# A spectral filter and a GELU network on one core: ten tiles' sums kept instead of eight, side-by-side copies of leftover rows, and a new written order

## The chip, the cores and the metric

The kernel runs on one NeuronCore of a Trainium2 chip, as one launch. The metric is the device time of that launch in microseconds (us). Five engines work in parallel, each through its own instructions in order: TensorE (PE, matmuls; its weight loads are shown as PEld), VectorE (DVE), ScalarE (ACT), GpSimd (POOL) and SyncE (SP), which issues nearly all the transfers.

## The reference

The input x has 2048 rows of 640 numbers in bfloat16. It is normalised by row, and the result is the sum of x, of a spectral filter of the normalised rows and of a two-layer network of the same rows:

```python
xn = _layernorm(x, axis=-1)
# A: X = rfft2(xn) over rows and columns, X * (w_r + i w_i), irfft2 back, cast to bf16
# B: h = gelu(xn @ w1 + b1), with w1 640 x 1536;  h @ w2 + b2, with w2 1536 x 640
return x + _A_ref(xn, A_w_r, A_w_i) + _B_ref(xn, B_w1, B_b1, B_w2, B_b2)
```

## The kernel before

The 2048 rows are 16 tiles of 128 rows, row 16p + c lying in tile c on partition p. Everything on PE is a matmul with a 128x128 stationary operand (or a 32-row piece of one), and all of PE's work goes through the helper on line 410, so the profile shows PE by what goes in and out of it, not by line.

*The network.* The first layer runs over seven blocks of tiles (`BLOCKS`: tiles 0, 1, 2-3, 4-5, 6-7, 8-11, 12-15) and 12 chunks of 128 hidden units. `h5.7.0` is block 5, chunk 7, inner slices from 0: three matmuls `ps<-xnT,W`; `h5.7.3` is the other two. ACT applies the GELU (`ge5.7`, line 639). The second layer of a tile is 12 matmuls of 384 columns and 12 of 256 (`CUTS`), `ps<-W,gT`, written in trios: `l9.384.3` is tile 9, the columns from 384, chunks 3 to 5. What the first-layer results sit in is called a bank: PSUM has eight, numbered 0 to 7, and each name in `SLOTS` is given one. `xb`, `Y`, `os` and the like have slots in SBUF in the same list.

*The filter.* The transform over columns and rows is a chain of matmul stages, each with a copy or products behind it. `G` does the first part of the transform over rows (copies `gx` into XV). `b0` to `b5` do the transform over columns, one for each of six `GROUPS` of 3, 3, 2, 3, 3 and 2 tiles (24 or 16 matmuls, `ps<-EB,XV`; copies `xb`). `c0` to `c3` finish the transform over rows with 32x32 matmuls (copies `y`), DVE multiplies with the filter (`m`, lines 690 and 693, and `z`, line 699), `d0` to `d3` go back over the rows (`ps<-T,ntab`; copies `u`), and sixteen transposing transfers `vt0` to `vt15`, issued by SP on line 705, turn the result into XV. `e0` to `e5` (24 or 16 matmuls, `ps<-getab,XV`) are the way back over the columns, group by group; each needs all sixteen turns. Behind an `e` stand copies `yo` and sums `y2` and `yf`, and then for each tile a last matmul `fin` (`ps<-Wf,htab`), DVE's final addition `os` (line 806) and the transfer `out` (line 813).

In `b` and `e` the 160 frequencies do not fit 128 partitions. Each tile has four matmuls of 128 rows and four of 32 rows, the leftover rows, which sit together in the fifth slice of XV, rows of four sorts on four groups of 32 partitions.

*Kept and unkept tiles.* For a tile in `KEEP` the second-layer sums (`k` instead of `l`) are copied out of PSUM early, with x added (`kk`, line 796), into 32-bit space in xnT that the first layer has finished with. Its bank is then free; `fin` later goes to a fresh bank and `os` adds the two. For the others `l` and `fin` share one bank, which is held until `os`.

*Order and waits.* The order on each engine is not found at run time: `ORDER` writes it out, engine by engine, `SLOTS` gives the buffers, and a planner (`Plan`) only derives from the two which semaphore each instruction waits for. Each PSUM bank and slot is reused in the order written, so an instruction may wait for data, or for the last reader of the slot it writes.

## Time and profile before

| | |
|---|---|
| time before, median of 3 runs | 149.14 us (148.47 to 150.26) |
| time of the profiled execution | 148.87 us |
| its span, first to last instruction | 147.5 us |
| mean granted TensorE clock | 1.000 |
| PE busy | 141.7 us (96% of the span) |
| PE weight loads busy | 99.8 us (68%) |
| DVE busy | 114.7 us (78%) |
| ACT busy | 79.3 us (54%) |
| POOL busy | 7.2 us (5%) |

The time of a run is longer than the span by 1.37 us in this execution, which lies around it. [...] In a timeline of the trace a row gives the start, the length, the engine, what is written and read, and the number of instructions merged into it; the time between the starts of two rows, divided by the count of the first, is the pace.

### The profile page before, as it was taken

The page shows a single profiled execution, that of the slowest core. Times are in us where ns is not written, and L with a number is a line of the kernel's source. Part 1 is how long each engine was busy: PE and PEld are TensorE (multiplying, and loading weights), DVE is VectorE, ACT ScalarE, POOL GpSimd, SP SyncE. Part 2 cuts the span into 40 slices and gives each one's busy share as a digit, 9 for nine tenths or more (in the row PEclk, how much of TensorE's full clock was granted, in tenths as well). Part 3 has the DMA queues.
Part 4 walks back from the last instruction along what each step waited for, and adds up shares of the span by engine and source line. Part 5 has one row for each costly group of instructions (what it writes and reads, how often), then busy time and mean ns, then how long its engine had stood idle before and what let it go on. Part 6 is the DMA issues. An engine that isn't in the chain of part 4 may idle for free.

```text
span 147.5 us, 4149 instructions
## 1 busy us (share of the span) xinstructions
PE 141.7 (96%) x1751; PEld 99.8 (68%) x1760; DVE 114.7 (78%) x264; ACT 79.3 (54%) x149; POOL 7.2 (5%) x24
## 2 busy tenths in 40 slices
PE   7999999999999999999999999999899999999993
PEld 7899898886478867455364434446686786667882
DVE  2999999999997555798988999410488789296993
ACT  3659998979755734577795767655242102300000
POOL 2030204112000000000000000000000000000000
PEclk9999999999999999999999999999999999999999
DMA  4999869887999899000007685669001022012225
GB/s 135 306 354 408 142 141 343 145 101 137 293 155 160 221 201 266 16 4 0 7 0 57 126 118 99 103 131 94 2 0 49 0 78 102 5 44 89 89 93 178
DMA packets 29226, 18.40 MB, mean 125 GB/s; under 512 B 20248, under 2 KB 27928, under 8 KB 29080
## 3 DMA queue, kind: packets, MB, share of 16 engines
q1 hardware_dynamic: 29184, 18.14, 54.2%
q8 instruction: 14, 0.23, 0.6%
q14 instruction: 4, 0.03, 0.1%
q10 hardware_dynamic: 24, 0.00, 0.0%
HBM read 10.92 MB, written 2.62 MB: 92 GB/s over the span
## 4 chain that ended last, share of the span: by engine, by line
PE 86%; DMA 4%; ACT 3%; DVE 2%; SPq 2%; issue 1%
PE ps L410 85%; DMA XV<-U 2%; SPq L705 2%; ACT Xb L420 2%; DMA X<-in_A_x_dram 2%; DVE U L521 1%; ACT U L420 1%; PE ps L567 1%; ACT gT L639 0%; DVE T L553 0%; DVE W L806 0%; DVE mv L523 0%; DVE rstd L527 0%
## 5 line engine op out<-in xcount | busy, mean ns | idle before, releaser
L410 PE MATMUL ps<-W,gT 128*128 128x256 bf16 (+3 forms) x396 | 59.3, 296 | 0.0
L410 PE MATMUL ps<-xnT,W 128*128 128x256 bf16 (+2 forms) x411 | 55.5, 286 | 1.2 <-issue 1.1
L410 PEld LDWEIGHTS ps<-W,gT 128*128 128x128 bf16 x396 | 36.9, 98 | 15.4 <-issue 1.2
L410 PEld LDWEIGHTS ps<-xnT,W 128*128 128x128 bf16 x420 | 34.5, 98 | 16.0 <-issue 2.8
L639 ACT ACTIVATE gT<-ps,b1col 128x256 bf16<-128x256 f32 (+2 forms) x84 | 37.6, 524 | 10.3 <-PE ps L410 10.0
L420 ACT ACTIVATE Wf<-ps 128x960 bf16<-128x960 f32 (+1 forms) x8 | 6.7, 869 | 19.2 <-PE ps L410 15.7
L521 DVE BATCH_NORM_STATS2 U<-X 128x6 f32<-128x320 bf16 x32 | 14.1, 473 | 2.1 <-DMA X<-in_A_x_dram 2.1
L420 ACT ACTIVATE T<-ps 128x644 bf16<-128x644 f32 (+2 forms) x17 | 9.3, 580 | 4.7 <-PE ps L410 4.7
L796 DVE TENSOR_TENSOR xnT<-ps,X 128x384 f32<-128x384 f32 (+1 forms) x16 | 7.6, 486 | 4.8 <-PE ps L410 4.8
L806 DVE TENSOR_TENSOR W<-ps,xnT 128x384 bf16<-128x384 f32 (+1 forms) x16 | 7.5, 485 | 4.7 <-PE ps L410 4.5
L420 ACT ACTIVATE XV<-ps 128x1280 bf16<-128x1280 f32 (+1 forms) x8 | 9.6, 1202 | 2.0 <-PE ps L410 2.0
L421 DVE CAST Wf<-ps 128x960 bf16<-128x960 f32 (+1 forms) x4 | 4.3, 1073 | 7.1 <-PE ps L410 7.1
L584 DVE TENSOR_TENSOR T<-T 128x128 bf16<-128x128 bf16 (+1 forms) x32 | 8.9, 315 | 0.1
L806 DVE TENSOR_TENSOR W<-ps,X 128x384 bf16<-128x384 f32 (+3 forms) x17 | 7.6, 465 | 1.7 <-PE ps L410 1.6
L410 PE MATMUL ps<-Wf,htab 128*128 128x384 bf16 (+3 forms) x33 | 8.6, 296 | 0.0
L410 PE MATMUL ps<-getab,XV 32*128 32x160 bf16 (+1 forms) x128 | 7.5, 242 | 0.5 <-DMA XV<-U 0.5
L420 ACT ACTIVATE Xb<-ps 128x960 bf16<-128x960 f32 x5 | 6.2, 1260 | 3.4 <-PE ps L410 3.4
L410 PEld LDWEIGHTS ps<-getab,XV 32*128 32x128 bf16 (+1 forms) x128 | 6.7, 146 | 1.7 <-DMA XV<-U 0.8
L420 ACT ACTIVATE U<-ps 128x512 bf16<-128x512 f32 (+2 forms) x13 | 5.3, 475 | 4.4 <-PE ps L410 4.4
L699 DVE TENSOR_TENSOR T<-T 128x644 bf16<-128x644 bf16 x16 | 7.3, 487 | 0.2
L410 PE MATMUL ps<-EB,XV 32*128 32x160 bf16 (+1 forms) x128 | 7.2, 232 | 0.2 <-ACT Xb L420 0.2
L532 POOL TENSOR_TENSOR rstd<-ve,mhalf 128x2 f32<-128x2 f32 (+1 forms) x8 | 6.1, 758 | 26.6 <-DVE ve L531 26.6
(56 smaller groups left out, 124.6 us busy)
## 6 DMA issues: line engine op xcount, KB each, us to landing
out_dram<-W SPq DMA_DIRECT2D x15, 160.0 KB, 1.8
X<-in_A_x_dram SPq DMA_DIRECT2D x7, 320.0 KB, 5.8
W<-in_B_w_dram SPq DMA_DIRECT2D x10, 192.0 KB, 4.7
W<-in_B_w_dram SPq DMA_DIRECT2D x2, 960.0 KB, 7.0
Wf<-in_A_w_r_dram SPq DMA_DIRECT2D x7, 160.5 KB, 5.5
Wf<-in_A_w_i_dram SPq DMA_DIRECT2D x7, 160.5 KB, 3.8
gtab<-c_G SPq DMA_DIRECT2D x1, 512.0 KB, 7.5
htab<-c_H SPq DMA_DIRECT2D x1, 512.0 KB, 6.1
```

The lines of the kernel that those rows point to most:

```text
L410: ins = e.matmul(o_, lhsT=lw, rhs=rh, start=st, stop=sp_, skip_group_check=True)
L420: return e.activation(dst(), src(), ACT.Copy)
L421: return e.tensor_copy(dst(), src())
L521: K.op(f"st{c}.{h}", "dve", lambda e, _, c=c, h=h: e.bn_stats(stats[:, c, 6 * h:6 * h + 6], view(X, c * D + H2 * h, [[1, H2]])), reads=[B_ ...
L532: K.op(f"rs{c0}", "pool", lambda e, _, a=a, b=b: e.tensor_tensor(out=rstd[:, a:b], in0=ve[:, a:b], in1=mhalf[:, a:b], op=ALU.pow), reads=[ ...
L567: ins = e.transpose(psb(tps.slot, [[1, 512]]).bitcast(BF)[:, 128 * j:128 * j + 128], xnv(n, 128 * j, [[1, 128]]), ident)
L584: ring_ops.append(K.op(f"f2{pair}.{k}{i}", "dve", lambda e, _, op=op, x1v=x1v, xfv=xfv, o_=o_, o0=o0, o1=o1, w=w: e.tensor_tensor(out=xfv( ...
L639: K.op(f"ge{bi}.{fc}", "act", lambda e, _, c0=c0, nt=nt, fc=fc, f0=f0, hps=hps: e.activation(gT[:, fc, 128 * c0:128 * (c0 + nt)], psb(hps. ...
L699: return e.tensor_tensor(out=rows, in0=rows, in1=view(TT, TB.slot * 4 * KP + r * KP, [[2 * KP, 2], [1, KP]]), op=op)
L705: K.op(f"vt{q}", "sp", lambda e, _, q=q, qq=qq, U=Us[pair]: e.dma_start_transpose(XV[:, :, 128 * q:128 * q + 128], uv(U, D * qq, [[1, D]]) ...
L796: K.op(f"kk{c}.{o0}", "dve", lambda e, _, kps=kps, c=c, home=home, o0=o0, w=w: e.tensor_tensor(out=home[:, o0 // 128:(o0 + w) // 128], in0 ...
L806: K.op(f"os{c}.{o0}", "dve", lambda e, _, c=c, os_=os_, fps=fps, o0=o0, w=w, kept=kept, home=home if kept else None: e.tensor_tensor(out=( ...
```

## The change

- `KEEP` gains tiles 0 and 3. The existing code has two more homes for them, in the part of W1's space that no output slot uses, free once the whole first layer is done. So `l0` and `l3` become `k0` and `k3`, with four more copies `kk0.0`, `kk0.384`, `kk3.0`, `kk3.384`.
- For groups 2, 3, 4 and 5 (`NEAR`) a new operation `xr` copies the leftover rows of the group's tiles from XV, where neighbouring columns of the stationary operand stand 16 elements apart, into T with the columns side by side (384 or 256 columns). The 32-row matmuls of `e2` to `e5` load from there. `xr3` and `xr4` are put on ACT, `xr2` and `xr5` on DVE. The 128-row matmuls of those groups and all of `e0` and `e1` stay as they are.
- An operation no longer waits by semaphore for a table load that stands ahead of it on its own engine.
- `ORDER` and `SLOTS` are rewritten throughout. 23 copies change between ACT and DVE.

```diff
-            o.waits = [d for d in set(o.deps) if d.dma or d.eng != o.eng or o.eng != "pe"]
+            o.waits = [d for d in set(o.deps) if d.dma or d.eng != o.eng or o.eng != "pe" and d.name[:5] != "table"]
...
-KEEP = (1, 2, 4, 5, 7, 8, 10, 11)
+NEAR = (2, 3, 4, 5)
+KEEP = (1, 2, 4, 5, 7, 8, 10, 11, 0, 3)
...
-        p_yo, p_y2, p_yf, p_os = [Pool(k, n) for k, n in (("yo", 2), ("y2", 1), ("yf", 2), ("os", 4))]
+        p_yo, p_y2, p_yf, p_os, p_xr = [Pool(k, n) for k, n in (("yo", 2), ("y2", 1), ("yf", 2), ("os", 4), ("xr", 3))]
...
-            pe(f"e{gi}", lambda c0=c0, n=n, eps_=eps_: width(
-                eps_.slot, n, lambda i, g, p0, k: part(XV, p0, k, 2048 * g + c0 + i, [[16, 128]]), getab),
-                reads=B_v + [B_ge], writes=[eps_])
+            xr = K.buf(f"xr{gi}", p_xr) if gi in NEAR else None
+            if xr:
+                K.op(f"xr{gi}", "act dve", copy(lambda c0=c0, n=n, xr=xr: view(TT, 384 * xr.slot, [[128, n], [1, 128]]),
+                     lambda c0=c0, n=n: view(XV, 2048 * 4 + c0, [[1, n], [16, 128]])), reads=B_v, writes=[xr])
+            pe(f"e{gi}", lambda c0=c0, n=n, eps_=eps_, xr=xr: width(
+                eps_.slot, n, lambda i, g, p0, k: part(TT, p0, k, 384 * xr.slot + 128 * i, [[1, 128]]) if xr and g == 4 else part(XV, p0, k, 2048 * g + c0 + i, [[16, 128]]), getab),
+                reads=B_v + [B_ge] + ([xr] if xr else []), writes=[eps_])
```

The parts of the order that the prediction speaks of, PE alone: between `d3.0` and `e0` stood

```
h6.4 h6.10 k8.0.9 l3.0.0 h6.11 l3.0.3 h6.0 l3.0.6 l3.384 (4 trios) l0.0.0
```

and there now stand

```
k8.384.0 .3 .6 h6.8 k11.0.0 k0.0.0 k8.384.9 k0.0.3 k3.0.0 k3.0.3 k0.0.6 k11.0.3 k0.0.9 k11.0.6 k3.0.6
k3.384.0 k11.0.9 l6.0.0 k3.384.3 .6 .9
```

The turns are issued as 2, 3, 1, 7, 0, 6, 4, 5, 8, 9, 11, 10, 14, 15, 13, 12 before, and as 0, 1, 2, 4, 7, 3, 5, 6, 11, 10, 9, 8, 15, 14, 12, 13 now. The groups of the way back run as e0, e1, e3, e2, e4, e5 before, and as e0, e1, e4, e2, e3, e5 now. Copies of one stage on ACT and DVE before and now: `xb4.0` and `xb4.1` both on ACT, now DVE and ACT; `xb2` ACT and DVE, now both DVE; `xb3` DVE and ACT, now both ACT; `u7` both on ACT, now both on DVE; `u6` DVE and ACT, now both ACT. The second half of W2 (`w2_1`) is issued by SP as the fourth transfer after `td11`, now directly after it; the first matmul that reads it is `k1.0.6`. The last transfers were issued as out8, out15.0, out10, out15.320, out14, out15.480, and are now out8, out10, out14, out15.0, out9, out15.320, out15.480.

## The prediction

> **What bounds the kernel now.** I read the page first, then the chain that ended last, then PE's timeline. The page's shares:

> ```profile
> span 147.5 us, 4149 instructions
> PE 141.7 (96%) x1751; PEld 99.8 (68%) x1760; DVE 114.7 (78%) x264; ACT 79.3 (54%) x149; POOL 7.2 (5%) x24
> PE 86%; DMA 4%; ACT 3%; DVE 2%; SPq 2%; issue 1%
> ```

> PE is busy nearly throughout and holds 86% of the chain. So only three things can move the end: a stretch in which PE waits, a change in PE's own pace, and the tail behind its last matmul. The chain in order of time (start, length, what) names where PE was not the one that was late:

> ```profile
> 64.76 2.38 ACT Xb L420 x2
> ...
> 98.89 1.26 SPq L705
> ...
> 100.19 3.65 DMA XV<-U
> ...
> 103.89 41.09 PE ps L410 x375
> ```

> From 103.89 on the chain is PE without a break to the last copy. Ahead of that lie ACT's copies for b3 and the turns ahead of e0. PE's timeline gives the paces and the waits:

> ```profile
> 64.87 2.11 PE L410 MATMUL ps<-xnT,W 128*128 128x512 bf16 x9 [0.16 <-issue]
> 67.19 1.32 PE L410 MATMUL ps<-EB,XV 128*128 128x160 bf16 x24 [0.21 <-ACT Xb L420]
> 68.44 1.64 PE L410 MATMUL ps<-W,gT 128*128 128x384 bf16 x9
> ...
> 88.70 0.92 PE L410 MATMUL ps<-T,ntab 32*32 32x320 bf16 x32
> 89.55 2.33 PE L410 MATMUL ps<-xnT,W 128*128 128x512 bf16 x10
> 91.72 1.47 PE L410 MATMUL ps<-W,gT 128*128 128x256 bf16 x12
> ...
> 94.75 0.51 PE L410 MATMUL ps<-T,ntab 32*32 32x320 bf16 x32
> 95.20 2.33 PE L410 MATMUL ps<-xnT,W 128*128 128x512 bf16 x10
> ...
> 103.89 1.42 PE L410 MATMUL ps<-getab,XV 128*128 128x160 bf16 x24 [0.45 <-DMA XV<-U]
> ...
> 120.66 1.36 PE L410 MATMUL ps<-getab,XV 128*128 128x160 bf16 x24
> 121.95 0.45 PE L410 MATMUL ps<-Wf,htab 128*128 128x384 bf16 x2
> ...
> 126.22 1.64 PE L410 MATMUL ps<-W,gT 128*128 128x384 bf16 x9
> 127.69 0.33 PE L410 MATMUL ps<-Wf,htab 128*128 128x384 bf16 x1
> ...
> 136.33 1.47 PE L410 MATMUL ps<-W,gT 128*128 128x256 bf16 x12
> 137.64 0.27 PE L410 MATMUL ps<-Wf,htab 128*128 128x256 bf16 x1
> ```

> Start to start, a matmul of 512 columns takes (91.72 - 89.55)/10 = 0.217 us, one of 384 takes (127.69 - 126.22)/9 = 0.163, one of 256 takes (137.64 - 136.33)/12 = 0.109. Three waits stand out:

> - b3. Nine matmuls from 64.87 end their pace at 66.82, and b3 starts at 67.19: **0.37**. Both xb4 copies were on ACT, 2.38 us in a row.
> - Behind d2.1. The next row starts 0.85 after it; behind d3.0 it is 95.20 - 94.75 = 0.45: **0.40**. Nothing late is named; the weight loads call it issue, 0.66 where 0.25 is usual behind a d:

> ```profile
> 87.51 0.76 PEld L410 LDWEIGHTS ps<-xnT,W 128*128 128x128 bf16 x5 [0.25 <-issue]
> ...
> 89.55 1.84 PEld L410 LDWEIGHTS ps<-xnT,W 128*128 128x128 bf16 x10 [0.66 <-issue]
> ```

> - e0. Between d3.0 and e0 stood 20 matmuls of 512 columns, 15 of 384 and 12 of 256: 0.45 + 4.34 + 2.45 + 1.31 = 8.55 us of cover. e0 came 103.89 - 94.75 = 9.14 after d3.0: **0.59**.

> Together 1.36 us. Everything else is PE at its pace, or waits of some 0.1.

> **The change part by part.**

> *Ten kept tiles.* PE's matmuls are the same in number and size. What changes is that k0 and k3 no longer hold their banks until their fin, so more of layer two can stand ahead of e0. In the new order d3.0 is followed by 36 matmuls of 384, 24 of 256 and 5 of 512: 0.45 + 5.87 + 2.62 + 1.09 = 10.0 us. The chain to cover took 9.14: u7, then four turns of 1.26 to 1.28 on SP, then 3.65 to land. u7 moves from ACT to DVE, still ahead of the last four turns. So e0's wait goes, with some 0.8 in hand: -0.59 (nothing gained if the turns land 1.5 later, below). What is late next is PE itself.

> The price is four more copies on DVE:

> ```profile
> L796 DVE TENSOR_TENSOR xnT<-ps,X 128x384 f32<-128x384 f32 x8 | 4.3, 551 | 3.4 <-PE ps L410 3.4
> ...
> L796 DVE TENSOR_TENSOR xnT<-ps,X 128x256 f32<-128x256 f32 x8 | 3.3, 420 | 1.4 <-PE ps L410 1.4
> ...
> 103.90:145.40 41.50, 41.06 (x389) 30.96 (x389) 32.36 (x65) 6.74 (x8) 0.00 (x0) 1.00 0.15 55
> ```

> 2 x (0.551 + 0.420) = 1.94 us. The last row is the stretch behind e0: DVE was busy 32.36 of 41.5. By the paces, 3.9 us of matmuls that stood behind e0 now stand ahead of it, so the stretch shrinks to about 37. kk3.384, kk3.0 and kk0.384 add 1.4 there, kk11.0 leaves it, and two yo copies fewer stay on DVE: about 32 of 37. DVE still has room, so the four cost nothing; without that room they would cost their 1.94.

> *Leftover rows side by side.* Weight loads by shape, those of the way back (getab) and of b (EB), whose columns lie side by side:

> ```profile
> L410 PEld LDWEIGHTS ps<-getab,XV 128*128 128x128 bf16 x64 | 5.1, 144 | 1.2 <-DMA XV<-U 0.8 <-ACT Wf L420 0.2
> ...
> L410 PEld LDWEIGHTS ps<-EB,XV 128*128 128x128 bf16 x64 | 4.5, 98 | 1.6 <-ACT Xb L420 0.7 <-ACT U L420 0.4 <-DVE T L421 0.3
> ...
> L410 PEld LDWEIGHTS ps<-getab,XV 32*128 32x128 bf16 x64 | 1.6, 148 | 0.5
> ...
> L410 PEld LDWEIGHTS ps<-EB,XV 32*128 32x128 bf16 x64 | 1.0, 92 | 0.8
> ```

> A load of scattered columns takes 148 ns against 92. Little of it reaches PE's path: e4 with its 24 matmuls takes 121.95 - 120.66 = 1.29, b3 with as many 68.44 - 67.19 = 1.25. I take this 0.04 to 0.05 for each of four groups: **-0.18**, between 0 and -0.56 (56 ns for each of the ten sets of 32-row loads).

> [...]

> No row shows an xr. The nearest are PSUM copies of its width, the 551 ns above for 384 elements, and 1.16 us for 960 below; I take 0.55, between 0.2 and 1.2.

> ```profile
> 105.36 1.16 DVE L421 CAST Wf<-ps 128x960 bf16<-128x960 f32 x1 [6.75 <-PE ps L410]
> ```

> xr2 and xr5 lie where DVE sat idle 6.75 us ahead of yo0.1; they can start only when the last turn is in, with kk11.0 queued behind them, and yo0.1 behind that. With the turns in 0.8 ahead of e0 and yo0.1 due 1.4 behind its start, there are 2.2 us for 1.65. At 1.2 each, yo0.1 and with it e1 would be 0.7 late. ACT has 6.74 busy in 41.5 us: xr3 and xr4 are free.

> *The new order.* Adding up these paces along PE's new order I looked at each wait. xb4 is now split, but xb4.0 stands behind DVE's m3.1 and m0.1: of b3's 0.37 I keep 0.15 (0 to 0.37). The issue wait behind d2.1 has no cause that the order removes; I keep 0.15 of its 0.40 (0 to 0.40). The product stage on DVE is tight:

> ```profile
> 63.20:92.60 29.40, 28.28 (x490) 14.25 (x494) 27.63 (x47) 21.51 (x39) 0.15 (x2) 1.00 0.37 52
> ```

> From the first product to the last z DVE was busy 27.63 of 29.40. Now kk1.384 and kk8.0 fall into it: 28.6. By the paces d3 wants the last z 30.4 after the first product, so 1.8 is left for the idling that was 1.77 before. For this and a few banks that come free within 0.1 of their next use I add 0.15 (0 to 1).

> w2_1 goes out about 2 us earlier, but k1.0.6 reads it near 39.5, where it was 42.9:

> ```profile
> 27.57 4.54 SPq L559 DMA_TRANSPOSE xnT<-T  x3
> ...
> DMA to landing us min/median/max: 6.1/7.0/8.0
> ```

> Behind those turns' end at 32.1 it lands at 39.1 by the median of W2's two: nothing, or 0.6 by the largest.

> *The table waits.* Before the first GELU ACT waited 1.70 us for PE; the second table load, 1.28 us, now stands in that gap. Nothing.

> ```profile
> L529 ACT ACT_TABLE_LOAD x1 | 1.3, 1283 | 0.0
> ...
> 9.43 2.06 ACT L639 ACTIVATE gT<-ps,b1col 128x128 bf16<-128x128 f32 x7 [1.70 <-PE ps L410]
> ```

> *The tail.* SP's last eight issues:

> ```profile
> 140.49 5.79 SPq L813 DMA_DIRECT2D out_dram<-W x8
> ...
> 145.00 0.33 DVE L806 TENSOR_TENSOR W<-ps,X 128x160 bf16<-128x160 f32 x1 [0.22 <-PE ps L410]
> ```

> They end at 146.28, 0.95 behind the last copy, because out14 stood in front of out15.480. Now out14 goes earlier and out9 and out15.320 stand there: **-0.13** (0 to -0.35).

> *The sum*, against the profiled execution's own 148.87 (span 147.5 and 1.37 around it): -1.36 + 0.15 + 0.15 + 0.15 - 0.18 - 0.13 = -1.22, so **147.6 us**. The median shown, 149.14, lies 0.27 above that execution, within the runs' spread of 1.8; I leave the sum as it is. With all best ends the gain is about 2.1 (146.8), with all worst the case is a loss.

> **The rivals.**

> *All of it comes.* No new wait, no issue wait: 146.8. For it speaks that PE's waits were few and all named; against it that part of them had no visible cause. Chance 0.18.

> *The turns stay late.* The first turn now waits for u0.0, by the paces near 79.5; it was issued at 77.47. The fifteen steps from there to the last issue at 100.19 took 1.51 us each, more than the 1.26 of one alone. From 79.5 on they give a last issue at 102.2 and, 3.65 later, a landing at 105.8, e0's new place being 106.3 by the paces. If the steps take 1.6 us instead, which needs one more delay of 1.3 us, it lands at 107.1 and e0 waits 0.8: 148.4. Against it: the turns of the earlier pairs have waits of their own to give up. Chance 0.12.

> ```profile
> 77.47 3.48 SPq L705 DMA_TRANSPOSE XV<-T  x2
> ```

> *DVE's products become the bound.* Place: d3.1, behind z7.1. If DVE idles twice as long as before, 3.5 us, because it serves more alternating copies in order (xb2, u7, y2 and y3 changed engine), z7.1 is 28.6 + 3.5 = 32.1 behind the first product, 1.7 to 1.9 late, and all that follows with it: **149.5, slower than before**, 148.9 to 152 by the idling. It decides from an idling of 3.0 us, where the gain is gone. For it: 94% busy in that stretch; against it: the copies that changed engine balance nearly. Chance 0.15.

> *The side-by-side copies do nothing.* Without the 0.18 it is 147.8. The 148 against 92 ns of two loads of one shape speaks against it: 0.03. [...]

> **How the numbers follow.** The forecast has 0.46, with 146.9 to 148.5 for its own range. An order this different may also lose at a place that I have not found: 0.06, over 150. A measurement of this kernel can tell about 1% from no change, 1.5 us. Of the forecast about half, 0.24, lies beyond that, with the full gain 0.18: faster 0.42. Within 1%: 0.22 + 0.12 + 0.03 + 0.05 of the slower rival = 0.42. Slower: 0.10 + 0.06 = 0.16. The range 146.4 to 150.0 leaves out about 0.06 below and 0.13 above.

> **What would show it.** Right: no wait on XV's transfer ahead of e0; loads of 32-row shape out of T near 92 ns in e2 to e5, each of the four 0.04 to 0.05 shorter; 41.09 of unbroken PE behind e0 down to about 37; DVE's last z ahead of d3.1. Wrong: PE waiting in the stretch behind e0 for os or kk; PE waiting at d or c for DVE; k1.0.6 waiting for W2; an xr over 1 us.

## The result, and the profile after

The kernel after takes **148.24 us** (median of 21 runs, 147.29 to 149.55) beside 149.08 for the kernel before (21 runs, 148.47 to 150.28): a ratio of 0.9936, 95% interval 0.9912 to 0.996. Forecast were 147.6, within 146.4 to 150.0. The gain is real, but 0.84 us where the sum had 1.22. The profiled execution took 147.38 us and lies near the best end of the runs; the profile before was much nearer its median (148.87 beside 149.08). That difference turned out to be the main thing to explain.

The page and the chain in order of time:

```profile
span 146.1 us, 4167 instructions
PE 142.4 (97%) x1760; PEld 99.9 (68%) x1760; DVE 116.6 (80%) x272; ACT 79.7 (55%) x149; POOL 7.3 (5%) x24
PE 95%; DVE 2%; DMA 2%; issue 0%
```

```profile
13.20 46.73 PE ps L411 x485
59.93 83.62 PE ps L411 x1059
143.57 0.32 DVE W L811
```

ACT's copies and the turns, which the chain before named, are gone: from 13.20 to the last copy it is PE alone. PE's timeline at the three places of the prediction (one line number is shifted by one, L410 is now L411):

```profile
65.98 1.69 PE L411 MATMUL ps<-xnT,W 128*128 128x512 bf16 x7
67.50 1.31 PE L411 MATMUL ps<-EB,XV 128*128 128x160 bf16 x24
...
91.30 0.52 PE L411 MATMUL ps<-T,ntab 32*32 32x320 bf16 x32
91.74 3.19 PE L411 MATMUL ps<-xnT,W 128*128 128x512 bf16 x14
...
96.54 0.52 PE L411 MATMUL ps<-T,ntab 32*32 32x320 bf16 x32
...
106.55 1.36 PE L411 MATMUL ps<-getab,XV 128*128 128x160 bf16 x24
...
120.94 1.00 PE L411 MATMUL ps<-getab,XV 128*128 128x160 bf16 x12
121.87 0.39 PE L411 MATMUL ps<-getab,T 32*128 32x160 bf16 x12
122.19 1.15 PE L411 MATMUL ps<-W,gT 128*128 128x384 bf16 x6
```

b3 starts 1.52 us behind the start of seven matmuls of 0.217: no wait (their row lasts 1.69; PE's rows overlap). Behind d2.1 the next row comes after 0.44, where it was 0.85. e0 comes 10.01 after d3.0, the very cover that was worked out, with no idle bracket. So all three waits, 1.36 us, are gone in this execution, and none of their size has come in their place. e3 with its 24 matmuls takes 122.19 - 120.94 = 1.25, where e4, with as many, took 1.29 before.

DVE's product stage, the stretch behind e0 and the end of SP's queue:

```profile
64.63:94.55 29.92, 29.92 (x500) 14.92 (x500) 27.97 (x48) 21.49 (x39) 0.14 (x2) 1.00 0.29 51
...
106.55:143.90 37.35, 36.99 (x367) 28.17 (x365) 31.93 (x67) 9.19 (x11) 0.00 (x0) 1.00 0.17 63
```

```profile
135.76 9.12 SPq L818 DMA_DIRECT2D out_dram<-W  x10
...
143.57 0.32 DVE L811 TENSOR_TENSOR W<-ps,X 128x160 bf16<-128x160 f32 x1 [0.21 <-PE ps L411]
```

From the first product to the last z it was 29.92 us, 0.5 inside the 30.4 that d3 allows, with DVE busy 27.97. The stretch behind e0 is 37.35 (worked out: about 37) with DVE busy 31.93 of it (about 32). The tail has not moved: SP's last issue ends 144.88 - 143.89 = 0.99 behind the last copy, before 0.95.

### The profile page after: what moved, and what is told of

It is laid out like the page before. It is cut to its first block, busy times and chain, and to the rows that moved or that the text cites. A ratio compares the mean times of both kernels' runs of the same rounds, so it can differ in the third digit from the quotient of the medians.

```text
span 146.1 us, 4167 instructions
## 1 busy us (share of the span) xinstructions
PE 142.4 (97%) x1760; PEld 99.9 (68%) x1760; DVE 116.6 (80%) x272; ACT 79.7 (55%) x149; POOL 7.3 (5%) x24
## 3 DMA queue, kind: packets, MB, share of 16 engines
HBM read 10.92 MB, written 2.62 MB: 93 GB/s over the span
## 4 chain that ended last, share of the span: by engine, by line
PE 95%; DVE 2%; DMA 2%; issue 0%
PE ps L411 93%; DMA X<-in_A_x_dram 2%; DVE U L522 1%; PE ps L568 1%; DVE W L811 0%; DVE T L554 0%; DVE mv L524 0%; DVE rstd L528 0%
## 5 line engine op out<-in xcount | busy, mean ns | idle before, releaser
L411 PE MATMUL ps<-W,gT 128*128 128x256 bf16 (+3 forms) x396 | 58.8, 296 | 0.0
L411 PE MATMUL ps<-xnT,W 128*128 128x256 bf16 (+2 forms) x420 | 57.8, 288 | 0.0
L411 PEld LDWEIGHTS ps<-W,gT 128*128 128x128 bf16 x396 | 36.8, 98 | 15.3 <-issue 1.2
L411 PEld LDWEIGHTS ps<-xnT,W 128*128 128x128 bf16 x420 | 34.4, 98 | 15.2 <-issue 2.4
L640 ACT ACTIVATE gT<-ps,b1col 128x256 bf16<-128x256 f32 (+2 forms) x84 | 36.7, 522 | 8.5 <-PE ps L411 8.4
L421 ACT ACTIVATE Wf<-ps 128x960 bf16<-128x960 f32 (+1 forms) x9 | 7.6, 880 | 17.2 <-PE ps L411 17.2
L421 ACT ACTIVATE T<-ps 128x644 bf16<-128x644 f32 (+2 forms) x17 | 9.3, 581 | 8.0 <-PE ps L411 8.0
L421 ACT ACTIVATE XV<-ps 128x1280 bf16<-128x1280 f32 (+1 forms) x8 | 9.5, 1193 | 1.3 <-PE ps L411 1.3
L811 DVE TENSOR_TENSOR W<-ps,xnT 128x256 bf16<-128x256 f32 (+1 forms) x16 | 7.4, 481 | 1.4 <-DMA out_dram<-W 1.2
L554 DVE TENSOR_SCALAR T<-X,mv,rstd 128x640 bf16<-128x640 bf16 (+2 forms) x17 | 7.0, 433 | 1.6 <-POOL rstd L533 1.3
L422 DVE CAST T<-ps 128x644 bf16<-128x644 f32 x7 | 5.8, 828 | 2.9 <-PE ps L411 2.8
L421 ACT ACTIVATE Xb<-ps 128x960 bf16<-128x960 f32 x5 | 6.2, 1262 | 3.4 <-PE ps L411 3.4
L411 PE MATMUL ps<-Wf,htab 128*128 128x256 bf16 (+3 forms) x33 | 8.0, 296 | 0.0
L581 DVE TENSOR_TENSOR T<-T 128x640 bf16<-128x640 bf16 x16 | 7.3, 480 | 0.1
L411 PE MATMUL ps<-EB,XV 32*128 32x160 bf16 (+1 forms) x128 | 7.2, 232 | 0.0
L411 PEld LDWEIGHTS ps<-EB,XV 32*128 32x128 bf16 (+1 forms) x128 | 5.5, 95 | 2.2 <-ACT Xb L421 0.5
L774 DVE TENSOR_TENSOR Wf<-Wf 128x960 bf16<-128x960 bf16 (+1 forms) x12 | 6.8, 595 | 0.1
```

The lines of the kernel that those rows point to most:

```text
L411: ins = e.matmul(o_, lhsT=lw, rhs=rh, start=st, stop=sp_, skip_group_check=True)
L421: return e.activation(dst(), src(), ACT.Copy)
L554: norm = K.op(f"nm{c}" if not a else f"nm{c}.3", "dve", lambda e, _, c=c, n=n, a=a, b=b, xnv=xnv: e.tensor_scalar(out=xnv(n, a, [[1, b - a ...
L581: K.op(f"f1{pair}.{k}", "dve", lambda e, _, k=k, op=op, xnv=xnv, x1v=x1v: e.tensor_tensor(out=x1v(H2 * k, [[D, 2], [1, H2]]), in0=xnv(0, 0 ...
L640: K.op(f"ge{bi}.{fc}", "act", lambda e, _, c0=c0, nt=nt, fc=fc, f0=f0, hps=hps: e.activation(gT[:, fc, 128 * c0:128 * (c0 + nt)], psb(hps. ...
L774: K.op(f"yf{gi}.{k}", "dve", lambda e, _, k=k, op=op, y2=y2, yf=yf, n=n: e.tensor_tensor(out=view(Wf, YF + yf.slot * 3 * D + (D - 1) * k, ...
```

## The experiments

Each ratio is to the kernel before on the same chip, with its 95% interval.

**The kernel after, again.** No edit.

> The changed kernel, unchanged, profiled once more and timed. Its first profiled execution took 147.38 us, 0.86 less than its median of 148.24; before's took 148.87, 0.21 less than its median. Theory A (transfers arrive late in most runs): in the first profile the transposed tile 5 landed at 21.05 with its first reader at 21.15, tile 11 at 33.97 with its reader at 34.20, w2_1 at 38.66 with k1.0.6 at 39.62, and the last turn at 105.81 with e0 at 106.55. If these vary by some tenths from run to run, another profile shows PE waiting at one of these four places by 0.2 to 1 us, and the median stays near 148.2. Rival B (waits that no data explains, as the 0.40 behind d2.1 of before): the profile shows issue waits at no fixed place, and nothing at those four. Rival C (the first profile is typical and the spread lies around the span): PE again waits under 0.1 at each place, span 146.1, and the time above the span is what varies.

148.52 us median (12 runs, 147.71 to 150.42), ratio 0.9952 (0.9919 to 0.9986). This time the profiled execution took 149.09 us, in the upper half of the runs, and has a wait that the first lacks. PE's timeline, SP's, and the chain:

```profile
19.74 1.36 PE L411 MATMUL ps<-xnT,W 128*128 128x256 bf16 x11
22.45 0.82 PE L411 MATMUL ps<-xnT,W 128*128 128x256 bf16 x6 [1.34 <-DMA xnT<-T]
```

```profile
17.15 3.83 SPq L560 DMA_TRANSPOSE xnT<-T  x2
```

```profile
6.87 6.61 DMA X<-in_A_x_dram
13.51 1.67 DVE U L522 x4
...
16.68 0.80 DVE T L554 x2
...
19.72 2.64 DMA xnT<-T
22.45 13.19 PE ps L411 x136
```

The wait is at block 3's first matmul (tiles 4 and 5), on tile 5's transpose `td5`. By PE's pace (11 matmuls of 0.109 from 19.74) it is 1.5 us long, and nothing behind it gives it back: PE's other waits are as in the first profile. The two executions differ by 1.71, and two smaller things are in that too: here the first layer began 0.2 earlier, and SP's last issue ended 1.43 behind the last copy in place of 0.99. The chain tells where the lateness came from: the load of x for tiles 4 and 5 lands at 13.5, and statistics, normalising and the two transposes' issue follow. In the first profile the same pair of transposes stood so in SP's queue, with PE running through:

```profile
15.44 2.62 SPq L560 DMA_TRANSPOSE xnT<-T  x2
```

```profile
20.27 1.71 PE L411 MATMUL ps<-xnT,W 128*128 128x256 bf16 x14
21.82 0.44 PE L411 MATMUL ps<-gtab,T 128*128 128x128 bf16 x5
```

By the landings in the six traces of this order, x for tiles 4 and 5 came at 11.6 to 13.5 us and `td5` at 20.9 to 22.4; block 3 wants it at about 21. Theory A holds, with a wait longer than the 0.2 to 1 us that it gave.

**The leftover copies taken out.**

```diff
-NEAR = (2, 3, 4, 5)
+NEAR = ()
```

> The changed kernel with the four xr copies taken out: e2 to e5 load their leftover rows from XV again; order and slots else the same. Theory (side by side saves 0.04 to 0.05 us in each of four groups): e2, e3, e4, e5 take 0.95, 1.30, 1.30, 0.95 from first matmul to the next work instead of 0.90, 1.25, 1.25, 0.90, and the time is 0.1 to 0.2 us longer, ratio to the changed kernel 1.001. Rival (the copies cost more than they bring because xr2 and xr5 stand ahead of yo0.1 on DVE): the groups are longer but e1 starts earlier and the time is the same or shorter.

149.0 us (12 runs), ratio 0.9958 (0.9924 to 0.9993). This can't be told from the kernel after by time; the profile can tell. The 32-row loads are back at 148 ns, in the kernel after those out of T take 92:

```profile
L411 PEld LDWEIGHTS ps<-getab,XV 32*128 32x128 bf16 x64 | 1.6, 148 | 0.5
```

```profile
L411 PEld LDWEIGHTS ps<-getab,T 32*128 32x128 bf16 x40 | 0.6, 92 | 0.3
```

From an e's first matmul to the next operation's, e2, e3, e4 and e5 take 0.950, 1.294, 1.342 and 0.952 without the copies and 0.900, 1.249, 1.299 and 0.899 with them: 0.043 to 0.053 each, 0.19 together. (e4 has 0.05 more than e3, with the copies and without; what stands in it is open.)

**The copies alone, in the order before.**

```diff
+NEAR = (2, 3, 4, 5)
# xr2 xr5 ahead of yo0.1 on DVE, xr3 xr4 on ACT behind yo0.0 and yo3.1
```

> The kernel before with the xr copies alone, in its own order (xr2 and xr5 on DVE ahead of yo0.1, xr3 and xr4 on ACT behind the yo copies). Theory: e2 to e5 0.04 to 0.05 us shorter each, 0.18 in all, ratio to before 0.998 to 0.999; b3, d2.1 and e0 wait as before (0.37, 0.40, 0.59). Rival: no shorter, or yo0.1 late behind the copies (xr2 cannot start before the last turn has landed, when e0 starts too), which makes e1 late by up to 0.5.

149.65 us (12 runs), ratio 1.0021 (0.9997 to 1.0046). Each of the four e is again 0.046 to 0.050 shorter, 0.19 together, as forecast, and e1 starts 2.83 behind e0 as in before. The time doesn't show it: the 0.998 to 0.999 expected lie below the interval. In the profiled execution other things ate it (the first layer began 0.56 later than in before, most of that because PE was still at its slow pace, 0.107 us a matmul of 128 columns in `before_shift` where the full one is 0.056, on which the last section has more, and k1.0.6 waited some 0.45 for W2); why the median of the twelve runs shows no gain stays open. The wait behind d2.1 is the same as in before, although all of it comes 1 us later:

```profile
89.71 0.92 PE L411 MATMUL ps<-T,ntab 32*32 32x320 bf16 x32
90.56 0.82 PE L411 MATMUL ps<-xnT,W 128*128 128x512 bf16 x3
```

**Less cover ahead of e0.** `e0` moved to stand behind `k3.0.6`, with `k11.0.9` behind it, and on DVE `yo0.1` ahead of `kk11.0`.

> The changed kernel with e0 moved ahead of k11.0.9, k3.384 and l6.0.0, straight behind k3.0.6, so that the matmuls between d3.0 and e0 are 7.7 us instead of 10.0; the same matmuls run behind e0. Theory (the cover ahead of e0 is what took its wait away, and the turns are in some 9.3 us after d3.0): e0 waits 1.4 to 1.6 us for the last turn and the span is longer by as much, some 147.5. Rival (the turns come earlier in the new order and the cover is more than needed): e0 waits under 0.5.

150.06 us (10 runs), ratio 1.0017 (0.9978 to 1.0055): no gain over the kernel before is left to see. Of PE's timeline:

```profile
99.07 5.37 PE L411 MATMUL ps<-W,gT 128*128 128x384 bf16 x33
105.13 1.06 PE L411 MATMUL ps<-getab,XV 128*128 128x160 bf16 x12 [0.69 <-DMA XV<-U]
```

By the order 30 of the 33 have 384 columns and 3 have 256: they end their pace at 99.07 + 4.89 + 0.33 = 104.29, and e0 comes at 105.13, 0.84 later. That is less than the 1.4 to 1.6 expected: the last turn landed 8.5 us behind d3.0, where 9.3 had been taken from the first profile. The direction is that of the theory: with less cover in front, e0 waits.

**xb4 back on ACT.**

```diff
-dve:xb4.0 act:xb4.1
+act:xb4.0 act:xb4.1
```

> The kernel after with xb4.0 back on ACT, so that both copies of xb4 stand one behind the other there as before. By the prediction's term for b3: PE waits 0.3 to 0.4 us at b3 again (the bank is free 1.2 us later than with one copy on each engine, less the cover of the four h5 steps between b4 and b3). Rival: the new order has more in front of b3, and the wait is below 0.1.

149.13 us (one execution). PE and ACT:

```profile
66.44 1.69 PE L411 MATMUL ps<-xnT,W 128*128 128x512 bf16 x7
68.98 1.25 PE L411 MATMUL ps<-EB,XV 128*128 128x160 bf16 x19 [0.85 <-ACT Xb L421]
```

```profile
66.56 2.36 ACT L421 ACTIVATE Xb<-ps 128x960 bf16<-128x960 f32 x2 [0.54 <-PE ps L411]
```

Seven matmuls end their pace at 67.96, b3 comes at 68.98: 1.02, more than the 0.37 of before and than was expected. Between b4 and b3 stand seven matmuls in the new order, where it was ten by the order written (the row of before shows nine; a record is missing): 0.65 less of cover, and 0.37 + 0.65 is 1.02. So in this order the split was worth 1.0 us at b3 in this execution. (It also had 0.72 us at block 3: `td5`'s issue took 2.39 us there, not 1.27.)

**Tile 5's transpose covered.** The two group products stand in front of block 3's first matmul, as in before, and the first eight steps of block 3 run in two halves, tile 4's columns first.

```diff
+BYTILE = ((3, 4), (3, 6))
-pe:h3.6.0 ... pe:h3.4.0 ... pe:G3 ... pe:h3.6.3 ... pe:G2
+pe:G3 pe:G2 pe:h3.6.0.0 pe:h3.6.3.0 pe:h3.7.0.0 pe:h3.7.3.0 ... pe:h3.5.3.0 ... pe:h3.6.0.1 pe:h3.6.3.1
```

> The kernel after, with its two group products G3 and G2 placed ahead of block 3's first matmul, and the first eight steps of block 3 (inner blocks 6, 7, 4, 5) done in two halves, tile 4's columns first and tile 5's behind: tile 5's transpose is then needed 0.5 + 1.1 = 1.6 us later, for 20 more matmuls on PE (the same columns, about 0.05 us in all). Theory A (what the change still loses is a wait of 0 to 1.5 us for tile 5's transpose, which lands within 0.1 us of its first use in the best profile and 1.3 us late in a bad one): no wait at block 3 in the profile, the median falls from the 148.2 to 148.5 of the kernel after to 147.4 to 147.8 and the spread narrows. Theory B (the spread comes from elsewhere, and the transpose is late only now and then): the median stays at 148.2 to 148.6.

148.11 us (6 runs, 147.31 to 148.78), ratio **0.9897** (0.9859 to 0.9935). That is above the 147.4 to 147.8 of theory A, but the kernel before was slower on this chip as well, 149.64. PE runs through the place; 40 of the 42 matmuls in the second row are the halves of 128 columns:

```profile
20.89 0.72 PE L413 MATMUL ps<-gtab,T 128*128 128x128 bf16 x10
21.45 2.72 PE L413 MATMUL ps<-xnT,W 128*128 128x128 bf16 x42
```

> The kernel after unchanged, for the comparison on the same chip with the version that covers tile 5's transpose. Both theories: 148.0 to 148.6; in its profile a wait of 0 to 1.5 us at the first matmul of block 3.

The kernel after on the same chip: 149.04 us (12 runs, 147.62 to 149.92), ratio 0.9945 (0.9912 to 0.9979), and the wait is there again, 1.25 us by the pace:

```profile
20.74 0.38 PE L411 MATMUL ps<-xnT,W 128*128 128x256 bf16 x2
22.21 0.81 PE L411 MATMUL ps<-xnT,W 128*128 128x256 bf16 x6 [1.09 <-DMA xnT<-T]
```

> The version with tile 5's transpose covered, unchanged, a second time on another set of runs. Theory A: 0.988 to 0.992 of before (147.4 to 148.2 us beside 149.1 to 149.6), no wait at block 3 in the profile. Theory B (the first result was luck): 0.993 to 0.996 as for the kernel after.

The covered version a second time: 147.77 us (6 runs, 147.19 to 148.35), ratio **0.9887** (0.9843 to 0.993). Both profiled executions, 147.31 and 147.34 us, have no wait at block 3; `td5` landed at 20.87 and 21.31 in them, so neither shows the cover against a transpose as late as 22. Twelve runs in all have a median of 147.9, where the kernel after had 148.2 to 149.0; on the chip on which both ran it is 148.11 beside 149.04. Their lowest are the same as its lowest (147.2 beside 147.3), which is what taking away a wait that comes only in some runs should do. The spread narrowed to 1.6 us from 2.3 to 2.7: something else varies too.

**Only the two products in front.** G3 and G2 ahead of `h3.6.0`, no halves.

> The kernel after with G3 and G2 ahead of block 3's first matmul, where they stood in before, and nothing else: tile 5's transpose is needed 0.5 us later. Theory A: half a microsecond of the wait of 0 to 1.5 us goes, 0.990 to 0.994 of before, between the kernel after and the version with 1.6 us of cover; in the profile the wait at block 3 is 0 to 0.9 us. Theory B: as the kernel after, 0.993 to 0.996.

148.76 us (12 runs), ratio 0.9942 (0.9908 to 0.9977). By the ratio this is what theory B gave, and lies just outside theory A's 0.990 to 0.994. In its profile x for tiles 4 and 5 came at 13.9, the latest seen, and PE still waited 0.62 by the pace:

```profile
21.29 0.44 PE L411 MATMUL ps<-gtab,T 128*128 128x128 bf16 x5
22.19 3.22 PE L411 MATMUL ps<-xnT,W 128*128 128x256 bf16 x28 [0.46 <-DMA xnT<-T]
```

Half a microsecond of cover for a lateness of up to 1.5 didn't show in the median; whether it is worth nothing or 0.2 us can't be told from these runs. So this run doesn't confirm what the covered version suggests.

**The halves in the order before.** `BYTILE = ((3, 0), (3, 2))`, tile 4 first.

> The kernel before with the first eight steps of its block 3 (inner blocks 0 to 3) done in two halves, tile 4's columns first: tile 5's transpose is needed 1.1 us later than in before, where the profile has it land 0.48 us ahead of its use. Theory A (the late transpose hurts whichever order has little room; before has 0.5 us): before gains 0.1 to 0.4 us, ratio 0.997 to 1.000 (the 0.4 us behind d2.1 may go as well, since 20 more matmuls stand ahead of it in the stream, and then be taken by e0's wait). Rival (before's order is not hurt at all): 1.000 to 1.002.

149.5 us (12 runs), ratio 0.9994 (0.9967 to 1.0021): no verdict between the two. The halves brought a price of their own here: they fill a PSUM bank later, its GELU reads it later, and the next chunk that is written to this bank waits 0.54 by the pace.

```profile
20.82 3.27 PE L411 MATMUL ps<-xnT,W 128*128 128x256 bf16 x48
24.47 1.05 PE L411 MATMUL ps<-xnT,W 128*128 128x256 bf16 x8 [0.38 <-ACT gT L642]
```

**The wait behind d2.1: other places in the instruction stream.** First 32 idle matmuls at the start in place of 38, then 44, in the kernel before.

```diff
-WARM = (38, 4)
+WARM = (32, 4)   # and, in the other kernel, (44, 4)
```

> The kernel before with 32 matmuls in place of 38 in the row of idle ones that warm PE up before the first load lands: every later PE instruction stands 12 places earlier in PE's instruction stream, and nothing else changes. The wait of 0.40 us behind d2.1 sits in front of the last of its 32 matmuls (0.415 us between starts where 0.003 is usual), with no semaphore on that matmul. Theory P (it comes from the place in the instruction stream, where a dense run of 64 short instructions in 0.2 us outruns the supply): the wait is gone, from d2.1 to h6.3.0 0.45 us in place of 0.85, or it shows in front of another matmul. Theory S (it comes from what runs beside d2.1): it stays at 0.40 in front of the same matmul. Time 148.5 to 149.3 by P, 149.1 by S.

> The kernel before with 44 idle matmuls at the start in place of 38 (the run with 32 left PE at about half its pace for the first 24 matmuls of layer one, 1.2 us in all, and had no wait behind d2.1). Warm-up: PE at full pace from its first real matmul, h0 at 6.5 to 6.7 us, no loss there. Theory P (the wait behind d2.1 depends on the place in the instruction stream): it is gone, or sits in front of another matmul than the last of d2.1. Theory S (it went in the run with 32 because everything came 1.4 us later): here, with nothing later, 0.40 us in front of the last matmul of d2.1.

With 32 the wait is gone: d2.1 at 90.45, the next row 0.45 later. PE's timeline:

```profile
90.45 0.51 PE L410 MATMUL ps<-T,ntab 32*32 32x320 bf16 x32
90.90 1.47 PE L410 MATMUL ps<-xnT,W 128*128 128x512 bf16 x6
```

With 44 it stands inside d2.1, six matmuls earlier, and is 0.15 long. PE's weight loads:

```profile
89.26 0.17 PEld L410 LDWEIGHTS ps<-T,ntab 32*32 32x32 bf16 x26 [0.42 <-DVE gtab L421]
89.60 0.10 PEld L410 LDWEIGHTS ps<-T,ntab 32*32 32x32 bf16 x6 [0.17 <-issue]
```

Counting PE's matmuls from the first one by their weight loads, the wait is in front of number 1233 each time: the 32nd of d2.1 in before, the 26th with 44, the 12th in the version of before with the halves (20 more matmuls ahead of it; 0.155 between starts). With 32, that matmul is one of 512 columns, and nothing is seen. So in this order the wait goes with a place in the stream, as theory P has it; that a supply is outrun there, no run shows. The place alone is not enough, though: in the kernel after, matmul 1233 is the 18th of d2.1, and PE's weight loads there have no wait. The other six profiles of that order have none either.

```profile
91.30 0.19 PEld L411 LDWEIGHTS ps<-T,ntab 32*32 32x32 bf16 x32 [0.42 <-ACT T L421]
91.74 1.19 PEld L411 LDWEIGHTS ps<-xnT,W 128*128 128x128 bf16 x7 [0.25 <-issue]
```

(Neither run's time serves for more. With 32 the first layer was slowed, as told below; with 44 PE waited 1.6 us for an output buffer at the last tile.)

## Why the prediction was right, and where it was not

*The three waits (-1.36).* They are gone in full, for b3 and e0 by the mechanism of the forecast, behind d2.1 by luck. The forecast kept 0.15 of b3's, and that step was too careful: no wait is left there, and `b3_act` shows that the split decides it. It kept 0.15 behind d2.1 because "no cause that the order removes" was known, and none is known now. In the kernel before the wait goes with one place in the instruction stream; in the new order the same stage lies over that place and shows nothing.

*e0 and the turns.* Right to the hundredth in the cover (10.0 worked out, 10.01 in the trace); in the first profile the last turn landed at 105.81, with 0.74 in hand. `less_cover` shows the other side. The 0.59 itself is one execution's: in the order before, e0 waited 0.61 in `near_only`, 0.48 with 44 idle matmuls, and not at all with the halves, where the last turn took 2.65 to land in place of 3.65. The rival of the late turns did not happen, but that the landing came out at the 105.8 worked out is luck: the issues took 1.57 us a step from 79.69 on, not 1.51, close to the 1.6 with which the rival decides, and the last turn landed 2.63 behind its issue, not 3.65.

*DVE's tight places (+0.15).* Nothing of it is seen: 29.92 us for the product stage (busy 27.97, where 28.6 had been worked out), and the four more `kk` cost nothing on PE. `k1.0.6` did not wait for W2 either. The rival with DVE as the bound falls.

*Side-by-side copies (-0.18).* Right: 0.043 to 0.053 for each of four groups, in the traces; no median shows it. The copies were taken at 0.55. The two on DVE took some 0.39, right behind the last turn, and the two on ACT 0.90, within the bounds, and nothing waited for them:

```profile
105.83 0.69 DVE L422 COPY T<-XV 128x256 bf16<-128x256 bf16 x2 [1.45 <-DMA XV<-U]
```

```profile
L421 ACT ACTIVATE T<-XV 128x384 bf16<-128x384 bf16 x2 | 1.8, 904 | 0.0
```

The rival by which they do nothing falls: the loads went from 148 to 92 ns with the columns side by side. (They also read T in place of XV; but the loads of b have their columns side by side in XV and take 92 too.)

*The tail (-0.13).* Wrong, and this term failed as a step: out14 went away from in front of the last output, but out9 and out15.320 took its place and were issued back to back with it, at 143.47, 143.95 and 144.42. Three issues of some 0.45 end 0.99 behind the copy as before. It was read as one issue fewer, where it was one in another's place. Nor is the tail fixed: in the seven profiles of the new order, those of the covered version aside, it was 0.96 to 1.73 us. It grew with the time that `out10` took to land, which was 3.1 to 3.9 us in them, where most outputs take 1.75.

*The sum.* In the profiled executions the step is 148.87 - 147.38 = 1.49: the three waits 1.36, the copies 0.18, the tail -0.04, to 0.01. (The first layer began 0.25 later than in before, because PE was at its slow pace, 0.102 us for each of the first transposes, until 6.6; smaller waits of some 0.1, now gone as well, made up for it.) Of the ends of the sum, the best ones add up to a gain of 2.27, or 146.6, not to the 2.1 and 146.8 that stand there.

*What was missing.* The sentence "Adding up these paces along PE's new order I looked at each wait" did not hold for block 3. In before, G3 and G2 stood in front of its first matmul, and `td5` landed 0.48 ahead of its use; in the new order they stand behind it, which takes 0.5 us of cover away. In two of the six traces the transpose now lands 0.1 ahead of its use, in the others 0.2 to 1.5 behind. That the sum was made against one execution hid it further: with a transfer that varies by 1.5 us, a cover of 0.1 is no cover, and the forecast's median should have stood above its own profile by part of that. By these traces this wait, and the tail to a lesser part, turned the 1.49 us of the profile into 0.84 in the medians. The covered version, which has the change's gains without this wait, has a ratio of 0.989, some 1.6 us. That the wait is what it takes away is likely, not shown: half a microsecond of cover alone gained nothing that could be seen, and in both of its profiles `out10` landed in 1.75 us, so some of the gain may lie in the tail.

What stays open: the 1.6 us of spread that the covered version still has. The outputs' landing is one part of it by the traces: the tail varies with it, and the execution with 44 idle matmuls lost 1.6 us at the last tile while two outputs took 3.8 and 3.4 us to land. No run changed it.

## What to carry to other kernels

For an order written out by hand, list what each early transfer is needed for and how much cover it has, by its latest landing seen and not by that of one profile: a rewritten order can gain 1.4 us of waits that show and lose some of it, here likely 0.7, in one that shows only in some executions. Profile the same kernel twice before explaining a median. And where a first step needs two transfers, letting the half that needs only the first go ahead costs some 0.06 us on PE by the paces here (40 matmuls at 0.056 in place of 20 at 0.109), if the bank that it holds longer is not wanted next; where it was, in the order before, the next chunk waited 0.54.

## What the runs showed of the hardware

*Transfers with a packet of kind instruction beside them took longer.* The pages before and after list a queue of that kind with 14 packets; the page before:

```profile
q8 instruction: 14, 0.23, 0.6%
```

*A wait at one place of PE's instructions.* The wait was found in front of matmul 1233, and a smaller one, of 0.01 to 0.15 us, within c3.0 in front of 1107: 126 apart, and 256 instructions by PE's records. In most of PE's work, at 0.05 to 0.22 us for a matmul, such a step can't be seen; in a stage of 32 matmuls that start 3 to 7 ns apart it was up to 0.41 us. What PE waits for there is open. That it was one of the packets above is not shown: in the kernel before, one had landed at 87.87, a microsecond ahead of the wait, and the next set out at 90.46; and the kernel after has no wait at the same places.

*The start of PE's full pace.* In the kernel before, with 38 idle matmuls, PE had full pace from its first transposes on, 0.058 us a matmul. With 32 it stood idle 0.97 us ahead of them, where it was 0.29, and was slow from there on, at 0.102. PE's timeline, and two stretches of layer one (length, PE's busy time and matmuls, the granted clock the last but two):

```profile
5.66 0.71 PE L567 MATMUL ps<-EB,T 128*128 128x128 bf16 x5 [0.97 <-DVE T L553]
```

```profile
7.13:9.65 2.52, 2.52 (x26) 2.52 (x25) 2.19 (x8) 1.05 (x3) 0.00 (x0) 1.00 1.03 356
9.69:12.00 2.31, 2.31 (x44) 2.31 (x42) 2.24 (x9) 0.75 (x3) 1.25 (x2) 1.00 1.05 399
```

24 matmuls of 128 columns took 0.107 us each, then 0.056: 1.2 us lost, while the column of the granted clock says 1.00 in both. The start of the full pace is not the same in every execution: by the starts of PE's matmuls, with 38 or 44 idle ones it lay between 4.2 and 6.9 us in thirteen profiles, with 32 at 9.7 in one. That the six idle matmuls less decided it is likely, from one execution. In the kernel after, with 38 and no such gap, the first transposes were slow too, 0.102 us a matmul by the next row's start at 5.97:

```profile
5.46 0.72 PE L568 MATMUL ps<-EB,T 128*128 128x128 bf16 x5
```
